# Sparse attention with a gated feed-forward: key tiles that hold their own 64 keys first, with the neighbours' rims copied on chip

## The chip, the cores and the metric

One core of a Trainium2 chip. The time is the device time of one execution in microseconds (us), as a median over the fast runs. The clock that the matrix engine (TensorE) is granted differs between executions: its mean over one execution of the kernel before was 0.984 to 0.994 of full speed. The engines are VectorE (DVE in the profile), ScalarE (ACT), GpSimd (POOL) and SyncE (SP). TensorE is PE, and its weight loads are PEld.

## The reference, cut to what matters

```python
B, H, S, D = 4, 8, 768, 64;  block, window = 32, 16
k_sum = k.reshape(B, H, S // block, block, D).max(axis=3)       # block maxima
v_sum = v.reshape(B, H, S // block, block, D).mean(axis=3)      # block means
local  = q @ k.T / 8,   kept where |i - j| < window
coarse = q @ k_sum.T / 8 + log(block)
x = softmax([local, coarse]) @ [v, v_sum]                       # 3072 x 512, all heads side by side
y = x + sigmoid(x @ w_res) * ((gelu(x @ w_gate) * (x @ w_val)) @ w_out)
```

A query sees the 31 keys within 15 positions of it, and 24 block keys. The feed-forward (w_gate, w_val: 512 x 1536, w_out back) has nearly all the arithmetic.

## The kernel before

Queries go in tiles of 64. The key tile of a query tile therefore holds 96 keys, its own 64 and a rim of 16 on each side, and below these the 24 block keys. In the kernel before these 96 rows lie in their natural order, and they are loaded whole: each rim row is read from memory a second time.

```python
def v_window(b, t):
    lo, hi = max(0, t * QT - WIN), min(S, t * QT + QT + WIN)
    r0 = lo - (t * QT - WIN)
    return r0, r0 + hi - lo, v[b, :, lo:hi, :].rearrange("h p d -> p h d")

def v_loads(b):                                   # 12 loads, f32 to bf16, issued by GpSimd
    for t in range(NT):
        r0, r1, src = v_window(b, t)
        nc.gpsimd.dma_start(out=vext[b % 2][r0:r1, t, :, 0:D], in_=src)

def k_place(b, hp, tp):                           # batches 0 and 1: tp is the turned k in PSUM
    nc.scalar.copy(<tiles 1..10 of kW, 96 keys each>, <tp>)
    nc.vector.tensor_copy(<tile 0>, <tp>);  nc.vector.tensor_copy(<tile 11>, <tp>)
    k_blocks(b, hp)                               # maxima by VectorE, then their copy into kW (L207)

def vsum_mm(b, vs, lo, hi):                       # block means of batch 0 on TensorE
    for t in range(lo, hi):
        for i in range(2):
            nc.tensor.matmul(vs[i][96:128, 0:DM // 2], bmat[:, t, :], vext[b % 2][0:BAND, t, 4*i:4*i+4, 0:D], ...)
```

The head of the kernel (batch 0, first half) turns k and q, makes four score tiles s with their exp P, makes the block means vs, copies them into vext (`vsum_head`), makes the four attention products ao, and then the first gate matmul g can run. keep_warm are idle matmuls that hold up the clock. The body (`fo_step`) makes g and vv for each of 12 columns of the feed-forward, and `res_step` and `ffn_step` make r and f. In odd units of a batch, the next batch is prepared inside these steps:

```python
for fo in range(0 if u else 2, FO):
    fo_step(st, gvT, fo)
    ...
    if half == 1 and nb < B:
        if fo == (4 if nb == 1 else 0):
            vsum_grp(nb, ps_t, "t")               # means: matmul, cast, four small copies by SyncE
            for i in range(4):
                vsum_bc(nb, 3 * i, 3 * i + 3, nc.gpsimd)      # into vext, GpSimd, 1.47 us each
        if nb == 1:
            if fo < NP: k_step(nb, fo, ps_t, "t") # turn k on TensorE, place it, maxima
        elif 4 <= fo < 4 + NP:
            k_blocks(nb, fo - 4)                  # maxima of batches 2 and 3
```

The softmax here doesn't subtract the row's maximum and nothing guards it: scores larger than these inputs give would overflow.

## Time and profile before

| | |
|---|---|
| time, median of 4 runs | 279.42 us (279.06 to 280.24) |
| span in the profiled run | 278.3 us |
| TensorE busy | 95% |
| first s, first ao, first g | 11.66, 21.26, 25.64 us |
| granted clock from 17.7 to 24.5 us | half |

A line of the timeline has the start, the length, the engine, the source line, and what was written and read; the bracket at its end says how long the engine sat idle before it and what released it. Such waits on TensorE, once the g and vv matmuls run back to back, are what can be saved. In the first 26 us everything can be saved that lies on the way to the first g. The lines are in the prediction.

### The profile page before, as it was taken

Reading aid. Unit: us, or ns where it says so; the run is one execution under the profiler, and the core shown is the slowest. Engines: PE = TensorE matmul, PEld = TensorE weight load, DVE = VectorE, ACT = ScalarE, POOL = GpSimd, SP = SyncE. Lnnn points to the kernel's source line nnn. Section 1 sums busy time; section 2 is a strip of 40 time slices with the busy share of each in tenths; the row PEclk is TensorE's granted clock in tenths of the full one; section 3 lists DMA queues with packets and bytes.
Section 4 is the critical chain, followed back from the end, with each engine's and each line's share of the span. In section 5 each row is a group of like instructions: output and inputs, shape, how many; then the busy total and the mean of one; then the engine's idle time right before and its main releaser. Section 6 shows DMA issues by size and latency. Waiting matters only on the chain.

```text
span 278.3 us, 5822 instructions
## 1 busy us (share of the span) xinstructions
PE 265.1 (95%) x2370; PEld 143.4 (52%) x2370; DVE 163.3 (59%) x366; ACT 129.8 (47%) x204; POOL 103.5 (37%) x130
## 2 busy tenths in 40 slices
PE   6879999999999999999899999999899999999994
PEld 2435554554544555455445565455454565556543
DVE  5847433599337633575956833685947743683424
ACT  1865447475466445543254445443255336343320
POOL 7986763520499962001999820001600000000000
PEclk9977999999999999999999999999999999999999
DMA  5999999994069999971199999311001100111003
GB/s 89 171 175 196 196 206 207 157 159 107 4 41 147 172 152 121 158 134 41 10 115 152 179 172 156 95 46 44 0 0 40 75 2 0 39 40 40 0 0 114
DMA packets 99818, 27.51 MB, mean 99 GB/s; under 512 B 83720, under 2 KB 96848, under 8 KB 99792
## 3 DMA queue, kind: packets, MB, share of 16 engines
q0 software_dynamic: 80560, 16.85, 69.6%
q1 hardware_dynamic: 19232, 10.30, 18.4%
q8 instruction: 18, 0.29, 0.4%
q14 instruction: 8, 0.07, 0.1%
HBM read 33.69 MB, written 6.29 MB: 144 GB/s over the span
## 4 chain that ended last, share of the span: by engine, by line
PE 83%; DVE 6%; DMA 5%; issue 2%; ACT 1%; POOL 1%; POOLq 0%; DVEq 0%
PE g L312 21%; PE f L344 21%; PE vv L312 20%; PE r L334 8%; PE ao L290 4%; PE s L272 3%; DMA q_sb<-in_q_dram 3%; PE xp L301 2%; DMA vext<-in_v_dram 2%; DVE ks L203 2%; DVE gvT L318 2%; PE tp L229 1%; PE f L365 1%; PE wp L373 1%; PE vs L250 1%
## 5 line engine op out<-in xcount | busy, mean ns | idle before, releaser
L318 DVE TENSOR_TENSOR gvT<-ge,vv 128x384 bf16<-128x384 f32 x96 | 52.6, 552 | 56.6 <-PE vv L312 56.1
L317 ACT ACTIVATE ge<-g 128x384 f32<-128x384 f32 x96 | 47.1, 491 | 82.6 <-DVE gvT L318 42.9
L312 PE MATMUL vv<-xT,w_val 128*128 128x384 bf16 x384 | 78.4, 326 | 2.8 <-DVE gvT L318 2.7
L312 PE MATMUL g<-xT,w_gate 128*128 128x384 bf16 x384 | 80.0, 326 | 0.1
L344 PE MATMUL f<-w_out,gvT 128*128 128x512 bf16 x276 | 65.5, 379 | 0.0
L312 PEld LDWEIGHTS <-w_val 128*128 128x128 bf16 x384 | 37.5, 98 | 29.0 <-issue 4.9
L312 PEld LDWEIGHTS <-w_gate 128*128 128x128 bf16 x384 | 35.7, 98 | 24.5 <-issue 2.5
L262 POOL COPY vext<-vsum 32x1536 bf16<-32x1536 bf16 x14 | 20.0, 1465 | 72.4 <-DMA vsum<-vpart 72.3
L276 ACT ACTIVATE P<-s,bias_t 128x768 bf16<-128x768 f32 x32 | 28.9, 902 | 31.9 <-PE s L272 31.7
L112 POOL DMA_DIRECT2D vext<-in_v_dram x48 | 36.6, 780 | 16.7 <-DMA w_out<-in_moe_w_out_dram 5.3
L344 PEld LDWEIGHTS <-gvT 128*128 128x128 bf16 x276 | 26.1, 98 | 29.3
L279 DVE TENSOR_TENSOR P<-P,maskt 128x768 bf16<-128x768 bf16 x32 | 17.8, 556 | 21.0 <-ACT P L276 20.9
L334 PE MATMUL r<-w_res,xT 128*128 128x512 bf16 x96 | 24.3, 380 | 0.0
L350 DVE SCALAR_TENSOR_TENSOR th<-th,f 128x512 f32<-128x512 f32 (+1 forms) x25 | 16.4, 658 | 6.1 <-PE f L344 5.8
L296 DVE TENSOR_TENSOR xn<-ao,rz 128x384 bf16<-128x384 f32 x32 | 17.8, 557 | 1.1
L120 POOL DMA_DIRECT2D k_nat<-in_k_dram x24 | 18.1, 768 | 0.0
L352 DVE SCALAR_TENSOR_TENSOR o<-th,xn 128x512 f32<-128x512 f32 (+1 forms) x25 | 16.8, 670 | 0.9
L294 DVE RECIPROCAL rz<-ao 128x6 f32<-128x6 f32 x32 | 6.2, 192 | 17.2 <-PE ao L290 17.2
L290 PEld LDWEIGHTS <-P 128*64 128x64 bf16 x384 | 9.0, 114 | 13.8 <-DVE P L279 6.4
L337 ACT ACTIVATE th<-r 128x512 f32<-128x512 f32 x24 | 14.2, 595 | 3.4 <-PE r L334 2.9
L203 DVE TENSOR_REDUCE ks<-kW 128x24 bf16<-128x768 bf16 x16 | 15.2, 948 | 0.3
L290 PE MATMUL ao<-vext,P 128*64 128x65 bf16 x384 | 12.6, 203 | 0.0
(71 smaller groups left out, 187.2 us busy)
## 6 DMA issues: line engine op xcount, KB each, us to landing
out_dram<-o SPq DMA_DIRECT2D x23, 256.0 KB
vext<-in_v_dram POOLq DMA_DIRECT2D x40, 96.0 KB, 6.6
k_nat<-in_k_dram POOLq DMA_DIRECT2D x20, 96.0 KB, 3.8
q_sb<-in_q_dram POOLq DMA_DIRECT2D x4, 384.0 KB, 8.6
w_gate<-in_moe_w_gate_dram POOLq DMA_DIRECT2D x6, 256.0 KB, 8.1
w_val<-in_moe_w_val_dram POOLq DMA_DIRECT2D x6, 256.0 KB, 8.7
w_out<-in_moe_w_out_dram POOLq DMA_DIRECT2D x3, 512.0 KB, 14.7
q_nat<-in_q_dram POOLq DMA_DIRECT2D x12, 128.0 KB, 6.0
```

What stands on the lines that cost most here:

```text
L112: nc.gpsimd.dma_start(out=vext[b % 2][r0:r1, t, :, 0:D], in_=src)
L120: nc.gpsimd.dma_start(out=k_nat[r0:r0 + hi - lo, t].rearrange("p (h d) -> p h d", d=D), in_=k[b, :, lo:hi, :].rearrange("h p d -> p h d"))
L203: nc.vector.tensor_reduce(out=ks.rearrange("d (t n) -> d t n", n=2), in_=kw[:, :, WIN:WIN + QT].rearrange("d t (n w) -> d t n w", w=BLK), ...
L262: eng.tensor_copy(vext[b % 2][96:128, lo:hi, :, 0:D], src)
L276: nc.scalar.activation(P.rearrange("p a t q -> p a (t q)"), s[:, :, 0:TU], AF.Exp, scale=scale, bias=bias_t[:])
L279: nc.vector.tensor_mul(Pf, Pf, maskt.unsqueeze(1).to_broadcast([128, 2 * HT, QT]))
L290: nc.tensor.matmul(ao[64 * e:64 * e + 64, sub, hh, :], P[:, hh, t, :], vext[b % 2][:, half * HT + t, 2 * hp + hh, 0:D + 1], start=True, st ...
L312: nc.tensor.matmul(ps[:, 0:TU], w[:, ko, fo * 128:(fo + 1) * 128], st["xT"][:, ko, :], start=(ko == 0), stop=(ko == KO - 1), skip_group_ch ...
L317: nc.scalar.activation(ge[:], g[:, 0:TU], AF.Gelu)
L318: nc.vector.tensor_mul(gvT[:, fo, :], ge[:], vv[:, 0:TU])
L334: nc.tensor.matmul(r[:], st["xT"][:, ko, ss], w_res[:, ko, :], start=(ko == 0), stop=(ko == KO - 1))
L344: nc.tensor.matmul(st["f", sub][:], gvT[:, fo, ss], w_out[:, fo, :], start=(fo == 0), stop=(fo == FO - 1), skip_group_check=True)
```

## The change

Its intent: to load each row of v and k once. The tiles hold their own 64 keys first (rows 0 to 63), and the two rims behind them (64 to 79 the following tile's first 16, 80 to 95 the preceding tile's last 16). The rims are copied on the chip. Since own rows start at row 0, the means need 64 rows only. The head's fillers are rearranged too.

```diff
-            nc.gpsimd.dma_start(out=vext[b % 2][r0:r1, t, :, 0:D], in_=src)
+            nc.gpsimd.dma_start(out=vext[b % 2][0:QT, t, :, 0:D], in_=v[b, :, t * QT:(t + 1) * QT, :]...)
+    def v_rims(b, lo, hi):
+        x = vext[b % 2]; a, e = min(hi, NT - 1), max(lo, 1)
+        nc.sync.dma_start(out=x[QT:QT + WIN, lo:a, :, 0:D], in_=x[0:WIN, lo + 1:a + 1, :, 0:D])
+        nc.sync.dma_start(out=x[QT + WIN:BAND, e:hi, :, 0:D], in_=x[QT - WIN:QT, e - 1:hi - 1, :, 0:D])
 # head: two of the mask's selects become four, and go behind the loads
-        <2 affine_selects on maskt, 2 on bpair>
         v_loads(0)
+        <4 affine_selects on maskt>
+        v_rims(0, 0, HT);  v_rims(0, HT, NT)
 # k of batches 0 and 1
-            nc.scalar.copy(<tiles 1..10, 96 keys>, <tp>)
-            nc.vector.tensor_copy(<tile 0>, <tp>);  nc.vector.tensor_copy(<tile 11>, <tp>)
-            k_blocks(b, hp)
+            nc.scalar.copy(kW[b % 2][:, :, hp, 0:QT]..., <tp, all 12 tiles, 64 keys>)
+            k_blocks(b, hp)
+            k_rims(b, slice(hp, hp + 1), nc.vector)          # two copies inside kW
 # k of batches 2 and 3: smaller load and DMA transpose, then
+                    k_rims(nb, slice(0, NP), nc.gpsimd)
 # means
-                                     vext[b % 2][0:BAND, t, 4 * i:4 * i + 4, 0:D],
+                                     vext[b % 2][0:QT, t, 4 * i:4 * i + 4, 0:D],
 # TensorE's order in the head
         vsum_mm(0, vs, 2, 5)
+        fill(2)
         s_step(0, 2, st)
+        fill(2)
         vsum_mm(0, vs, 5, 8)
+        fill(2)
         s_step(0, 3, st)
 ...
-        keep_warm(2); av_step(0, 0, st); keep_warm(2); av_step(0, 1, st, ps_mm, "mm"); keep_warm(1)
+        fill(3); av_step(0, 0, st, ps_mm, "mm"); fill(2); av_step(0, 1, st); fill(1)
 # later batches, in odd units, gate step 0
+                        v_rims(nb, 0, NT)
```

## The prediction

> **What bounds the kernel now.** I read the page first, then the busy table by stretches, the chain of waits, and the timelines of single engines where the chain leaves TensorE.
>
> ```profile
> span 278.3 us, 5822 instructions
> PE 265.1 (95%) x2370; PEld 143.4 (52%) x2370; DVE 163.3 (59%) x366; ACT 129.8 (47%) x204; POOL 103.5 (37%) x130
> ...
> PE   6879999999999999999899999999899999999994
> ...
> PEclk9977999999999999999999999999999999999999
> DMA  5999999994069999971199999311001100111003
> ```
>
> TensorE is the bound from slice 4 (28 us) to the end, and its matmuls there (g, vv, f, r) are untouched. Time can come only from the first 26 us, before the first g matmul, and from later places where TensorE waits. The table of stretches shows the start:
>
> ```profile
> core 0: us, PE busy (x) PEld busy (x) DVE busy (x) ACT busy (x) POOL busy (x), PEclk, DMA share, GB/s
> 10.90:14.30 3.40, 2.94 (x58) 1.97 (x59) 3.23 (x10) 3.29 (x6) 3.40 (x5) 1.00 2.41 153
> 14.30:17.70 3.40, 1.52 (x22) 0.92 (x20) 1.55 (x3) 1.77 (x3) 2.54 (x4) 1.00 2.33 160
> 17.70:21.10 3.40, 3.29 (x24) 1.44 (x22) 1.43 (x4) 2.72 (x4) 3.37 (x5) 0.50 1.50 194
> 21.10:24.50 3.40, 3.40 (x43) 1.73 (x42) 2.04 (x5) 1.94 (x4) 2.24 (x4) 0.50 1.45 195
> ```
>
> TensorE is busy 45% from 14.3 to 17.7 and then runs at half clock for 6.8 us. The timeline of TensorE says why, and the chain of waits confirms it (6.58 us of waiting on a v load, ending at 18.88):
>
> ```profile
> 17.47 0.38 PE L237 MATMUL vs<-vext,bmat 96*32 96x256 bf16 x2 [1.72 <-DMA vext<-in_v_dram]
> 17.78 0.50 PE L272 MATMUL s<-qT,kW 64*128 64x64 bf16 x12
> 18.24 2.13 PE L237 MATMUL vs<-vext,bmat 96*32 96x256 bf16 x8
> 20.30 1.03 PE L373 MATMUL wp<-warm 128*128 128x512 bf16 x2
> 21.26 0.54 PE L290 MATMUL ao<-vext,P 128*64 128x65 bf16 x12
> ...
> 25.64 0.49 PE L312 MATMUL g<-xT,w_gate 128*128 128x384 bf16 x2
> ```
>
> Block means need all 12 v tiles, and these land late. From GpSimd's timeline, the first seven v loads follow q at once; the eighth waits:
>
> ```profile
> 10.78 3.82 POOL L112 DMA_DIRECT2D vext<-in_v_dram  x5 [0.59 <-DMA q_sb<-in_q_dram]
> ```
>
> Later, TensorE waits in two kinds of place: some 0.24 us after each of four k turns of batch 1 (59 to 67 us), and 1.37 us at 136 and at 198:
>
> ```profile
> 61.12 0.53 PE L196 MATMUL tp<-ident,k_sb 96*64 96x96 bf16 x16 [0.24 <-DVE kW L220]
> 137.73 0.81 PE L312 MATMUL vv<-xT,w_val 128*128 128x384 bf16 x4 [1.37 <-DVE gvT L318]
> ```
>
> **What the Trainium skill says.** "TensorE: Matmul & The Clock Gate", part 1, says that the array drops to half clock after an idle window of about 3.4 us and comes back after a busy one. The trace agrees in kind: 0.50 for 6.8 us after a poorly filled stretch (it was not fully idle). "DMA: Bandwidth & Descriptors", "Queues, rings and completion order", says that each DMA engine takes turns between its queues by packets; so copies from SyncE share with loads from GpSimd. No run so far shows the size. "SBUF — State Buffer", "SBUF: two separate sides", says that VectorE and GpSimd lock each other out of a shared port pair. The trace agrees: the VectorE copy L207 takes 0.23 us alone and 1.21 and 1.48 us while GpSimd copies vext (131.4 to 137.1). Its "Door 1: The DMA port swizzle" puts a 64-partition load at 196 GB/s against more for wider ones; v moves at 154 now, so I expect no new limit.
>
> **The change, part by part.**
>
> *v loads.* A load shrinks from 96 to 64 rows, 98 KB to 65.5 KB written. From 10 to 17 us the queues move 154 GB/s, 0.64 us per old load; at the same rate a new one takes 0.43 us. Data of the 12 starts at about 10 us (q lands at 10.5). Old: 1147 KB / 154 = 7.45 us, so 17.4, and the last landing is about 19.4 (the load whose landing ends the chain's wait at 18.88 was issued at 12.30; the last went out at 13.85, and no load took under 5.6 us from issue to landing). New: 786 KB / 154 = 5.1 us, so 15.1. GpSimd still issues the last five from 10.78 at 0.76 us each, so the last is out at 14.6: about the same limit. With the 2 us that landing trailed the data before, the last v is there at about 17.1, plus up to 0.6 us from the rim copies in the queues: 17.1 to 17.7.
>
> *Rims of v.* Two SyncE copies per half, about 700 pieces of 128 B each, 44 per DMA engine. Old v loads took 48 pieces per engine in 0.64 us, so I estimate 0.6 us per copy alone and 1.2 shared. Tile seven lands at about 14.5; issue 0.66 us each (the time of a vsum copy on that queue), about 1.6 us to land (vsum copies: last issue ends 72.1, reader starts 73.7): 17.5 to 18. The first attention product needs the first half only. So rims just miss being the path.
>
> *Means and softmax side.* Old: vs ends at 20.30, ao starts at 21.26 (0.96 later: cast 0.43, first head 0.36, hand-overs). New: vs ends at 17.3 to 17.9. But the fourth s waits for tile eight (I put it at 15.5), two fillers and 0.35 us of s, then exp 0.90 and mask 0.56, so VectorE is free for the cast at about 17.9: ao at 18.7 to 18.9. The mask is made after the v issues now (four selects of 0.25 us from 14.6, ready at 15.6), so three mask products run at 15.6 to 17.2: hidden. Gain to here: 21.26 - 18.8 = 2.45 us.
>
> *Clock.* Six new fillers of 512 columns (0.22 us at full clock, 0.43 at half) stand at 14 to 17 us. 1.3 us of them in 3.4, plus 1.5 us of other work, makes about 80%, as in 10.9 to 14.3, which wasn't throttled. From ao to g took 4.38 us at half clock. At full clock VectorE's chain sets it: ao 0.38, then rz plus xn at 0.76 each, three of them, 0.6 us of hand-overs and xp: 3.2 us. Gain 1.2 us. The fillers behind vs (3 x 0.22 = 0.65) fit in the 0.96 us gap.
>
> Start in sum: 2.45 + 1.2 = 3.65. I weigh in one chance in five that the clock drops all the same (minus 1.2 or more): 3.4 us.
>
> *Do the weights follow?* w_res is there at about 39.9 and w_out's first third at 42.4 (GpSimd's waits end then), needed at 43.4 and 45.2. A start 3.6 us earlier needs them at 39.8 and 41.6. Their queue moves up by 1 to 2.3 us (fewer v bytes, minus rims). 38.3 and 40.7 would do; the margin is under 1 us.
>
> *k of batch 1.* Two copies from PSUM (0.15 us of VectorE's pace each, 0.23 long) go; two rim copies of 176 elements come, estimated 0.12 each against 0.15 to 0.23 for the 288 of L207. What matters more: the turned tile is now read by ScalarE alone (768 columns instead of 960, an estimated 0.78 us instead of 0.96), so TensorE's next turn no longer waits on VectorE's L220. VectorE's pace goes from 2.02 to about 1.84 us per step, TensorE's work is 1.77. Four waits of 0.24 go: 0.9 us.
>
> *k of batches 2 and 3.* Load and DMA transpose shrink by a third (12.35 and 9.2 us before), both hidden. Rims are two GpSimd copies of 704 elements per partition, at 1465 ns / 1536 elements an estimated 0.7 us each; they come near 108 us, when GpSimd has finished its loads, with nothing waiting. The block maxima on VectorE are the same size, and GpSimd's vext copies still collide with them: the two 1.37 us waits stay. Later v rims precede vsum's copies on SyncE and may push the collision by 1 us or so: 0 +- 0.8.
>
> Sum: 3.4 + 0.9 + 0 = 4.3 us, 279.6 to 275.3.
>
> **Rivals.**
> (a) The rim copies take the place of the v landing: SyncE copies queued among weight loads land after 19 us. For it: piece count hardly falls (2944 removed, 2816 added), and the queues are saturated. Against it: the first half needs only seven tiles. Gain at the start then 1.5 to 2: about 277.
> (b) The clock still drops, because the remaining waits on tiles 8 and 12 fall into one window. Fillers speak against it. About 276.8.
> (c) The weights become the bound in 35 to 46 us and give 1 us back: 276.3. The narrow margins speak for it, the 8-deep issue ahead against it.
> (d) The collisions at 133 and 195 shift out of the maxima entirely: 1.37 twice, about 272.7. It needs some 5 us of delay for vsum, which 2.4 us of rim traffic don't give.
>
> **Range and chances.** Errors of 1 us in landing, 0.8 in clock, 0.8 in collisions, 0.3 in k add up to about 1.6 us, more towards less gain. Predicted 275.3 us, range 273.7 to 277.5. 2% would be 274.0: faster by over 2% 0.15, within 2% 0.82, slower by over 2% 0.03.
>
> **What would show it.** Right: first g at about 22 us; clock 1.00 through 14 to 25; vs done before 18; no wait on L220 and none of 0.24 us at 56 to 64; waits of about 1.4 us before vv twice, DMA transpose of k near 8 and 6 us; TensorE without gaps at 35 to 46. Wrong: an ao waiting on a vext copy from SyncE (a), clock 0.50 (b), r or f waiting on w_res or w_out (c), or only one or no such wait before vv (d). A slower kernel would need the rims to hold ao past 21 us.

## The result, and the profile after

| | before | after |
|---|---|---|
| time, median of 4 runs | 279.42 us | 277.89 us (277.64 to 278.24) |
| ratio, 95% interval | | 0.9942 (0.9916 to 0.9969) |
| span in the profiled run | 278.3 us | 276.5 us |
| first ao, first g, first f | 21.26, 25.64, 45.17 us | 20.04, 23.23, 44.08 us |

A ratio is the mean time of one kernel's fast runs over that of the other's of the same rounds, so not quite the ratio of the medians quoted. Executions over 1.5% slower than the fastest of the same kernel are left out of the means. The gain is 1.5 us (0.6%, clear of noise) where 4.3 was forecast; 277.89 us lies just above the forecast range. Two rows of the page come first, the granted clock and the DMA share in 40 slices of the span:

```profile
PEclk9999999999999999999999999999999999999999
DMA  5999999999089999104099997104001100111003
```

The clock does not fall in this run. The busy table of the same stretches as before (columns: the stretch, TensorE, its weight loads, VectorE, ScalarE, GpSimd, clock, DMA share, GB/s):

```profile
10.90:14.30 3.40, 2.88 (x59) 1.92 (x58) 2.67 (x8) 3.33 (x6) 3.40 (x6) 1.00 2.21 143
14.30:17.70 3.40, 3.24 (x41) 1.52 (x40) 1.58 (x3) 1.59 (x4) 3.21 (x8) 1.00 1.22 113
17.70:21.10 3.40, 2.53 (x36) 1.42 (x35) 2.40 (x6) 3.31 (x5) 3.40 (x5) 1.00 1.31 158
21.10:24.50 3.40, 3.16 (x56) 2.01 (x49) 2.92 (x11) 2.55 (x6) 2.37 (x4) 1.00 1.59 196
```

Two things are to be read. TensorE is busy 95% from 14.3 to 17.7 where it was 45%: it no longer waits for v, and part of the time is now filled with idle matmuls (wp below). And the last column: before, the queues moved 160 and 194 GB/s in the two middle stretches, now 113 and 158. Less data was asked for, and the queues did not use the room. The timeline of TensorE:

```profile
16.71 0.61 PE L393 MATMUL wp<-warm 128*128 128x512 bf16 x2
17.25 0.35 PE L267 MATMUL s<-qT,kW 64*128 64x64 bf16 x12
17.53 1.04 PE L232 MATMUL vs<-vext,bmat 64*32 64x256 bf16 x8
18.50 0.82 PE L393 MATMUL wp<-warm 128*128 128x512 bf16 x3
20.04 0.38 PE L285 MATMUL ao<-vext,P 128*64 128x65 bf16 x12 [0.71 <-DVE vext L238]
...
23.23 0.49 PE L307 MATMUL g<-xT,w_gate 128*128 128x384 bf16 x2
...
36.15 0.36 PE L224 MATMUL tp<-ident,q_sb 96*64 96x96 bf16 x8 [0.82 <-DMA q_sb<-in_q_dram]
...
44.08 1.90 PE L339 MATMUL f<-w_out,gvT 128*128 128x512 bf16 x8 [0.29 <-DMA w_out<-in_moe_w_out_dram]
```

No bracket on vs, so v is there when TensorE comes to it. The fourth s at 17.25 stands behind fillers (wp). And at 36.15 and 44.08 stand waits on loads that the kernel before does not have. From the first g to the first f TensorE took 45.17 - 25.64 = 19.53 us before and takes 44.08 - 23.23 = 20.85 now: of 2.41 us gained at g, 1.32 are given back. The larger of the two named waits, 0.82 us, is on the second half's q, whose load GpSimd issues between the weights. GpSimd's own waits tell when weights land (before it issues another load it is seen waiting for an old one). Before:

```profile
40.16 0.77 POOL L112 DMA_DIRECT2D vext<-in_v_dram  x1 [1.73 <-DMA w_res<-in_moe_w_res_dram]
42.70 0.77 POOL L112 DMA_DIRECT2D vext<-in_v_dram  x1 [1.77 <-DMA w_out<-in_moe_w_out_dram]
```

After, with the mask's selects ahead of the first weight:

```profile
14.05 1.18 POOL L164 TENSOR_SCALAR_AFFINE_SELECT maskt<-maskt 64x64 bf16<-64x64 bf16 x4
15.22 0.77 POOL L177 DMA_DIRECT2D w_gate<-in_moe_w_gate_dram  x1
...
42.08 0.68 POOL L104 DMA_DIRECT2D vext<-in_v_dram  x1 [2.29 <-DMA w_res<-in_moe_w_res_dram]
44.31 0.68 POOL L104 DMA_DIRECT2D vext<-in_v_dram  x1 [1.56 <-DMA w_out<-in_moe_w_out_dram]
```

So the weights land 1.9 and 1.6 us later than before, although 360 KB less of v stood ahead of them. As many bytes of rim copies came in their place, and yet the queues moved less in all: from 13 to 22 us, 137 GB/s on average where it was 175. In the later stages, the maxima of batch 2:

```profile
133.02 5.72 POOL L257 COPY vext<-vsum 32x1536 bf16<-32x1536 bf16 x4 [24.29 <-DMA vsum<-vpart]
```

```profile
136.52 0.81 PE L307 MATMUL g<-xT,w_gate 128*128 128x384 bf16 x4 [0.23 <-DVE gvT L313]
139.34 0.81 PE L307 MATMUL g<-xT,w_gate 128*128 128x384 bf16 x4 [1.37 <-DVE gvT L313]
```

Counted from the means matmul of that stage, GpSimd's copies start 133.02 - 123.65 = 9.37 us in, where they started 131.43 - 125.50 = 5.93 us in before. SyncE, which issues the rims and then the four copies of the means, shows why. Before and after:

```profile
127.21 2.85 SPq L256 DMA_DIRECT2D vsum<-vpart  x4
```

```profile
126.37 5.30 SPq L251 DMA_DIRECT2D vsum<-vpart  x4
```

The copies of the means start 2.72 us after the means matmul instead of 1.71, behind two rim copies, and take 5.30 us instead of 2.85. GpSimd's copies then collide with other maxima than before, at the same price: from the means matmul to the next unit's first s the two stages took 16.88 and 16.80 us before and take 17.09 and 16.80.

### The profile page after: what moved, and what is told of

The parts are those of the page before. It is cut to its first block, busy times and chain, and to the rows that moved or that the text cites. A ratio compares the mean times of both kernels' runs of the same rounds, so it can differ in the third digit from the quotient of the medians.

```text
span 276.5 us, 5854 instructions
## 1 busy us (share of the span) xinstructions
PE 262.2 (95%) x2352; PEld 142.7 (52%) x2377; DVE 161.9 (59%) x365; ACT 128.7 (47%) x204; POOL 101.2 (37%) x134
## 4 chain that ended last, share of the span: by engine, by line
PE 75%; DMA 11%; DVE 4%; POOL 4%; issue 3%; ACT 1%; POOLq 0%; DVEq 0%
PE f L339 20%; PE g L307 19%; PE vv L307 18%; PE r L329 7%; DMA w_out<-in_moe_w_out_dram 5%; DMA w_gate<-in_moe_w_gate_dram 4%; PE ao L285 3%; PE s L267 3%; DMA q_sb<-in_q_dram 3%; PE xp L296 2%; DVE ks L199 2%; DVE gvT L313 2%; POOL vext L104 1%; PE f L360 1%; PE tp L224 1%
## 5 line engine op out<-in xcount | busy, mean ns | idle before, releaser
L339 PE MATMUL f<-w_out,gvT 128*128 128x512 bf16 x262 | 62.6, 379 | 1.6 <-issue 1.0
L104 POOL DMA_DIRECT2D vext<-in_v_dram x48 | 33.1, 761 | 13.3 <-DMA w_out<-in_moe_w_out_dram 5.3
L274 DVE TENSOR_TENSOR P<-P,maskt 128x768 bf16<-128x768 bf16 x32 | 17.7, 556 | 20.6 <-ACT P L271 18.9
L117 POOL DMA_DIRECT2D k_nat<-in_k_dram x24 | 16.4, 746 | 0.0
```

Of the source, the lines that this page charges most:

```text
L104: nc.gpsimd.dma_start(out=vext[b % 2][0:QT, t, :, 0:D], in_=v[b, :, t * QT:(t + 1) * QT, :].rearrange("h p d -> p h d"))
L274: nc.vector.tensor_mul(Pf, Pf, maskt.unsqueeze(1).to_broadcast([128, 2 * HT, QT]))
L339: nc.tensor.matmul(st["f", sub][:], gvT[:, fo, ss], w_out[:, fo, :], start=(fo == 0), stop=(fo == FO - 1), skip_group_check=True)
```

## The experiments

All ratios are against runs of the kernel before on the same chip in the same rounds. The interval is 95%. Where medians of two experiments are compared, they can come from different chips, on which the kernel before took 279.3 to 279.6 us. Each landing time is that of one profiled execution. Runs 3, 5 and 6 leave the loads of the head as the change has them, and there GpSimd's waits on w_res and w_out end at 41.21, 41.70 and 41.81, and at 43.73, 43.94 and 44.35 us, against 42.08 and 44.31 in the profile after. So a landing time is sure to about 0.9 us only.

**1. Without the rim copies of v in batch 0.** Wrong result on purpose: ScalarE zeroes those rows early.

```diff
+        nc.scalar.copy(vext[0][QT:BAND, :, :, 0:D], <zeros>)
-        v_rims(0, 0, HT);  v_rims(0, HT, NT)
```

> The changed kernel without the two pairs of on-chip rim copies of batch 0 (those rows zeroed by ScalarE early, so the result is wrong on purpose). Theory 1, the rim copies' traffic holds up the weight loads: the second q load and w_res, w_out land 1.2 to 2.5 us earlier than in the changed kernel (w_out's first third at 41.5 to 42.8 instead of 44.0), TensorE's wait of 0.8 us before the first turn of the second q half goes, and the span is about 1.2 us shorter: near 276.5 us against 277.9. Theory 2, the queue runs dry because GpSimd issues the first weight late (15.22, after four mask selects): weights move by under 0.5 us and the time stays at 277.5 to 278.

Measured: ratio 0.9935 (0.9906 to 0.9964), median 277.84 us, but six runs from 276.12 to 280.82, the longest of them slow. GpSimd's waits on w_res and w_out end at 41.05 and 43.59, so 1.0 and 0.7 us earlier than in the profile after: more than theory 2 allowed and less than theory 1 asked. The wait of 0.8 us for the second half's q is gone, and the span is 0.9 us shorter. But against run 3, which keeps the rims and issues its first weight at the same time (15.02 against 15.01), the weights come only 0.16 and 0.14 us earlier: what the rims alone cost is not settled. The busy table of this run by single microseconds shows the other half of it:

```profile
13.00:14.00 1.00, 0.44 (x20) 0.39 (x19) 0.97 (x4) 0.93 (x3) 1.00 (x3) 1.00 2.29 157
14.00:15.00 1.00, 1.00 (x15) 0.66 (x12) 1.00 (x2) 1.00 (x2) 0.81 (x4) 1.00 1.38 83
15.00:16.00 1.00, 1.00 (x16) 0.34 (x14) 0.96 (x6) 0.40 (x2) 1.00 (x3) 1.00 1.12 71
16.00:17.00 1.00, 1.00 (x8) 0.48 (x7) 0.73 (x3) 0.72 (x1) 1.00 (x2) 1.00 0.40 25
17.00:18.00 1.00, 1.00 (x17) 0.51 (x17) 0.31 (x1) 0.07 (x1) 1.00 (x3) 1.00 1.36 183
```

With the rims gone nothing hides it: the small v loads are through by 16 (about 1980 KB have moved by then; k, q and v have 1966), the first weight was issued from 15.01 to 15.78, and from 16 to 17 the queues move 25 GB/s. The queue runs dry. By the same count the larger v loads of the kernel before last until about 17, and the first weight was issued at 14.59.

**2. The mask's selects ahead of the v loads.**

```diff
         q_sb[0] = load_q(0, 0)
+        <4 affine_selects on maskt>
         v_loads(0)
-        <4 affine_selects on maskt>
```

> The changed kernel with GpSimd's four mask selects ahead of the v loads instead of behind them (where the kernel before has its selects). Theory 2 (queue dry for want of issue): first weight issued about 1.2 us earlier, at 14.0, w_out's first third lands at 42.8 to 43.2 instead of 44.0, waits at 36 and 44 us shrink, time about 277.0. Theory 1 (rim traffic): nothing moves at 36 to 44, 277.9.

Measured: the first weight is issued at 13.86, and the waits end at 41.06 and 43.60: again 1.0 and 0.7 us earlier than in the profile after, in the direction of theory 2, but again only 0.15 and 0.13 earlier than in run 3. The time did not follow: ratio 0.9977 (0.9945 to 1.001), runs from 277.6 to 280.8. In the profiled run ao waited 0.27 us on a rim copy, and the clock fell to 0.54 from 21.1 to 24.5. That weights which come earlier stand beside the rims in the queues is a guess, not shown. So theory 2 may be right on the weights, its time was missed, and the clock is less safe than the profile after suggested.

**3. Without the six fillers.**

```diff
-        fill(2)
         s_step(0, 2, st)
-        fill(2)
         vsum_mm(0, vs, 5, 8)
-        fill(2)
         s_step(0, 3, st)
```

> The changed kernel without the six fillers between the third and the fourth s. Theory 3, the fillers now stand on TensorE's path and made ao start at 20.0 instead of the predicted 18.8: ao at 19.0 to 19.4; and the clock stays 1.00 since v lands early enough. If instead the v tiles set it, ao stays near 20.0, and the clock falls to 0.50 for one or two windows. Either way the time moves little, 277.5 to 278.5, if the weights bind from 36 us on.

Measured: ratio 0.9946 (0.9933 to 0.996), 278.10 us. The profiled run, at full clock:

```profile
18.53 0.38 PE L285 MATMUL ao<-vext,P 128*64 128x65 bf16 x12 [0.41 <-DVE vext L238]
...
21.62 0.49 PE L307 MATMUL g<-xT,w_gate 128*128 128x384 bf16 x2
...
25.65 0.82 PE L307 MATMUL vv<-xT,w_val 128*128 128x384 bf16 x4 [0.37 <-DMA w_val<-in_moe_w_val_dram]
...
35.74 0.36 PE L224 MATMUL tp<-ident,q_sb 96*64 96x96 bf16 x8 [1.16 <-DMA q_sb<-in_q_dram]
```

ao starts 1.5 us earlier than in the changed kernel, and earlier than expected, and g 1.6. No wait for v shows on TensorE in the head even so. So the fillers stood on TensorE's path. But the first f came at 43.49, only 0.6 earlier, because TensorE now waits on loads, and in three of the five runs the clock averaged 0.984 to 0.987, as it does in most runs of the kernel before (the changed kernel, and runs 5 and 6 with the same head: 0.997 to 1.0 in all 13). In these runs the fillers do buy the clock, at 1.5 us; the time is the same without them (277.89 and 278.10).

**4. The kernel before, with only the changed kernel's TensorE order in the head.** Loads, key order and k as before.

> The kernel before with only the changed kernel's TensorE order in the head (nine more fillers of 512 columns and the swapped accumulators), loads and key order as before. If the clock is what the change gains at the start: clock 1.00 from 17.7 on, first g at 23.9 to 24.6 instead of 25.6, time about 278.2 (ratio 0.995), so as good as the whole change there. If the smaller v loads are what gains: still the wait on v until 17.5, g no earlier than 25, time 279.0 or more.

(It has seven more fillers; the text above miscounts.) Measured: ratio 0.9948 (0.9936 to 0.996), 278.01 us, at a mean clock of 0.998 to 1.0 in all five. That is as much as the whole effect of the change (0.9942), without the key order. Fillers and swapped accumulators were not tried apart. From its profile:

```profile
18.88 0.62 PE L237 MATMUL vs<-vext,bmat 96*32 96x256 bf16 x4 [0.19 <-DMA vext<-in_v_dram]
...
20.50 0.38 PE L290 MATMUL ao<-vext,P 128*64 128x65 bf16 x12 [0.24 <-DVE vext L243]
...
23.59 0.49 PE L312 MATMUL g<-xT,w_gate 128*128 128x384 bf16 x2
```

The wait on v shrank to 0.19 us, and g comes 0.36 us after the changed kernel's. f comes at 43.12, 0.96 before the changed kernel's, since the weights are not late here. What the key order earns later, with k of batch 1 (0.76 us), brings it level.

**5. The rims of k from PSUM.** In batches 0 and 1, VectorE takes them from the turned tile instead of from the placed keys.

```diff
-            k_rims(b, slice(hp, hp + 1), nc.vector)
+            nc.vector.tensor_copy(<first rims of kW>, tp.rearrange("d j (t p) -> d t p j", t=NT)[:, 1:NT, 0:2])
+            nc.vector.tensor_copy(<second rims>, tp.rearrange("d j (t p) -> d t p j", t=NT)[:, 0:NT - 1, 6:8])
```

> The changed kernel, but the rims of k in batches 0 and 1 are copied by VectorE from the turned tile in PSUM, as the kernel before does with its edge tiles, instead of from the placed keys. Theory: in batch 1 the changed kernel lost the four waits of 0.24 us because TensorE's next turn no longer waits for VectorE. Then the waits come back, at 176 elements per copy a little longer: 0.2 to 0.5 us each, 0.8 to 2 us in all between 57 and 66 us, time 278.7 to 279.8. If the gain came from the shorter ScalarE copy instead, no waits come back and the time is 277.9 plus at most 0.3.

Measured: ratio 1.015 (1.0134 to 1.0166), 283.69 us, 5.8 more than the changed kernel. The direction is as expected, the size is a miss:

```profile
60.84 0.53 PE L192 MATMUL tp<-ident,k_sb 96*64 96x96 bf16 x16 [1.41 <-DVE kW L219]
```

The waits are 1.41, 1.24, 1.24 and 1.24 us. My edit put the copies behind the maxima, so the PSUM tile stays held for the maxima too; in the kernel before the PSUM copies came first and held it less long (0.24 at the first turn). VectorE itself idles 1.00 us in each of the last three steps here, so its load is not the cause: who reads the turned tile last can set TensorE's next turn. In the kernel before, VectorE works without a pause from the second step on and takes 2.02 us for one; in the changed kernel it takes 1.82. How much of the old waits was its load, and how much the held tile, stays open.

**6. The maxima of batches 2 and 3 three steps earlier.**

```diff
-                    elif 4 <= fo < 4 + NP:
-                        k_blocks(nb, fo - 4)
+                    elif 1 <= fo < 1 + NP:
+                        k_blocks(nb, fo - 1)
```

> The changed kernel with the block maxima of batches 2 and 3 taken in the steps 1 to 4 instead of 4 to 7, so before GpSimd's copies into vext start. Theory: the two waits of TensorE there (1.6 and 1.0 us) come from VectorE's copy L203 being locked out by those copies. Then L203 takes 0.23 us in all eight places, the waits go to under 0.3 us each, and the time falls by 2 to 2.6 us to 275.3 to 275.9. If VectorE's sheer work makes the waits, they stay, and so does 277.9.

Measured: ratio 0.9825 (0.9806 to 0.9843), 274.70 us, and correct. No wait on TensorE is left in these stages, and the copy of the maxima takes 0.23 to 0.24 us in all eight places. From the means matmul to the next first s each stage takes 15.17 us instead of 17.09 and 16.80, which is 3.55 us in sum. That is more than the named waits (1.60 and 1.02) and more than expected: most of the rest is time that the profile counts as busy (15.49 and 15.64 us of TensorE in the changed kernel, 15.17 in both stages here, for the same matmuls). So GpSimd's copies blocked VectorE's, as the Trainium skill says that these two engines do in "SBUF — State Buffer", "SBUF: two separate sides": a VectorE copy that met GpSimd's copies took up to 1.48 us instead of 0.23, which is 1.25 more, a little under the 1.43 of one GpSimd copy. The last maxima end at 132.5; GpSimd's copies begin at

```profile
132.95 5.71 POOL L257 COPY vext<-vsum 32x1536 bf16<-32x1536 bf16 x4 [24.39 <-DMA vsum<-vpart]
```

**7 and 9. Runs 1 and 2 together, twice.**

> Runs 1 and 2 together: no rim copies of v in batch 0 (wrong result on purpose) and the mask selects ahead of the v loads. Each alone brought w_res about 1.0 us and w_out's first third about 0.7 us forward. If they are two separate causes, together they bring nearly the sum: the GpSimd waits on w_res and w_out end at 40.0 to 40.4 and 42.6 to 43.0 instead of 42.1 and 44.3, as in the kernel before or a little earlier. If both act on the same bottleneck (a queue that holds nothing from 14 to 17 us), no more than one of them: 41.0 and 43.6.

> Run 7's kernel once more, because its profile fell in the state with the lower clock. GpSimd's waits on w_res and w_out end where run 7 had them (39.7 and 42.2)[...]; if this execution keeps full clock, no TensorE wait on a load from 20 to 50 us and a span near 274.5.

Measured: the waits on w_res and w_out end at 39.66 and 42.20 in the first profile, 40.14 and 42.68 in the second. (Run 9 is a single execution.) That is about the sum, as in the kernel before, and clear of the scatter of the landing times. But both profiles fell in executions at half clock from about 14 to 25 us (mean clock 0.976), so I take it as a sign that the two causes add, not as proof. The timed runs are of two kinds: 275.8, 276.12 and 276.18 at full clock, and 279.26, 279.33 and 280.82 at a lower one (ratio 0.9919). At full clock that is 1.7 to 2.1 us less than the changed kernel takes, with spans of 274.1 to 274.5. Run 9 did not keep full clock, so the condition of its expectation was not met.

**8. The kernel before with runs 4 and 6.** TensorE's order in the head and early maxima, without the key order.

> The kernel before with the two things that helped apart from the key order: the changed kernel's TensorE order in the head (run 4) and the block maxima in steps 1 to 4 (run 6). Without the key order it keeps the four waits of 0.24 us on the k turns, but its weights come early. If run 4's 0.52% and run 6's gain of about 3 us add, 275.2 us, within 0.3% of run 6 (274.7): then the key order is worth next to nothing here. If the key order matters for the maxima (the rims now on GpSimd), 276 or more.

Measured: ratio 0.9892 (0.9877 to 0.9906), 276.56 us: a miss against 275.2. The two do not simply add:

```profile
129.48 5.70 POOL L262 COPY vext<-vsum 32x1536 bf16<-32x1536 bf16 x4 [21.32 <-DMA vsum<-vpart]
...
132.39 1.47 DVE L207 COPY kW<-ks 128x288 bf16<-128x288 bf16 x1
```

Without the rim copies, the means arrive early and GpSimd's copies start at 129.48, in the midst of the maxima, whose last copy then takes 1.47 us instead of 0.23. The stages take 16.12 and 16.05 us here, 1.83 more than run 6's in sum, about the whole difference between the two medians (1.86). With the early maxima, the key order is worth 0.9892 - 0.9825 = 0.7% after all, by the delay of 3.4 us that its rims bring to the means. That is luck, not the aim of the key order: an obvious rival, run 8 with the means simply made later, was not tried.

**10. A combination.** Run 6, with the selects first and the second half's rims of batch 0 issued by ScalarE in gate steps 3 and 5.

> A try to beat run 6 (274.7): its early maxima, the mask selects first, and the second half's rim copies issued by ScalarE in the gate steps 3 and 5, when TensorE has work, instead of by SyncE behind the v loads. Weights should come 1.2 to 1.5 us earlier than in the changed kernel (w_res 40.6 to 40.9, w_out 42.8 to 43.1). If the clock holds, 273.6 to 274.2; if it falls as in run 2 (where ao waited on the first half's rims), 275 to 276.

Measured: ratio 0.9826 (0.9803 to 0.985), median 274.41 us, runs from 273.66 to 275.45. The weights came 1.0 and 0.7 us earlier than in the profile after (41.06 and 43.61), a little later than expected, and the profiled run has a span of 272.3 against 273.0 in run 6, but two of six runs lost some clock (0.991, 0.994). So it is level with run 6. These two are the fastest versions found, 1.2% ahead of the changed kernel.

## Why the prediction was wrong, point by point

| step | forecast | measured |
|---|---|---|
| v no longer awaited | last v at 17.1 to 17.7 | SyncE's wait on v ends at 17.1; no TensorE wait on v |
| first ao | 18.7 to 18.9 | 20.04; 18.53 in run 3 |
| clock | full | full |
| ao to g | 3.2 us | 3.19 us |
| weights | 1 to 2.3 us earlier | 1.9 and 1.6 us later |
| k of batch 1 | 0.9 us gained | 0.76 us gained |
| second half's q | not listed | TensorE waits 0.82 us for it |
| later stages | 0 +- 0.8 us | 0.2 us lost |

**The head.** The mechanism was right and a term was too small. I let the fillers run "at 14 to 17 us" to fill idle time, set the fourth s by the landing of the eighth v tile, and counted two fillers behind it. In fact TensorE had no idle time left there; six fillers of 0.22 us stood in its order ahead of that s, and its exp and mask came before VectorE's cast of the means: the s ran at 17.25, and the cast at 19.16 where I had 17.9. Run 3, without them, has ao at 18.53 and g at 21.62, where the prediction put them (though its clock held in only two of five executions). The cost of the omission is 1.2 us at ao.

**The weights.** This step failed in its sign. "Their queue moves up by 1 to 2.3 us (fewer v bytes, minus rims)" takes it for granted that the queue is never empty: it counts bytes at a fixed rate. The runs show the opposite: the weights landed 1.9 and 1.6 us later, because the queues moved 137 GB/s from 13 to 22 us instead of 175. Smaller v loads were through before GpSimd, at 0.7 to 0.8 us per issue and with four selects in between, had given the queues a weight. Run 1 shows the hole (25 GB/s at 16 us). The selects' order (run 2) and the rims (run 1) each brought the weights 1.0 and 0.7 us forward against the profile after, but 0.1 to 0.2 against run 3, so the share of each is not settled. Both together (runs 7 and 9) brought them back to where the kernel before has them, which is clear of the scatter. The prediction's rivals (a), rims in the queues, and (c), weights as the bound, were the right ones to name; I gave them 277 and 276.3, and they came together. Rival (a) has a wrong count: 2816 pieces are removed, not 2944, exactly as many as one batch's rims add. And the first wait to bind, that for the second half's q, is in none of the lists. Run 1 also has a second dip at 20 us (112 GB/s) with no rims in it; what makes it stays open.

**k of batch 1.** TensorE's wait on VectorE went, as told: between the first turn and the next unit's first s, 19.78 us became 19.02. Only the first of the four waits had 0.24 us in its bracket: from one turn to what follows it, the steps took 2.17, 2.02, 2.02 and 2.02 us and now take 1.86 to 1.87. Run 5 shows that a VectorE read of the turned tile can set the pace.

**The later stages.** The sum was right, in part by luck. The delay was mis-sized: I expected the collision to move by about 1 us, and it moved by 3.4. It fell on two other maxima out of four, so nothing was gained. The 0.2 us are not firm either: with the same code there, run 3 has 16.80 and 16.81 us. Rival (d) said that a shift out of the maxima would be worth about 2.7 us but needed 5 us of delay. Run 6 made the same thing from the other side, and was worth 3.2 us. The delay is that of the rims in SyncE's order (1.0 us) and of the slower means copies behind them (5.30 us instead of 2.85), as its timeline shows; no run tests it alone.

**Where the expected gain went.** 3.65 us were expected at the first g (3.4 with the chance of a lower clock) and 2.41 came; at the first f 1.09 were left; 0.76 came from k; 0.2 were lost in the maxima: 1.6 us, against 1.8 between the two spans. And run 4 shows that TensorE's new order in the head (fillers and accumulators) is enough for nearly the whole gain there, without the smaller loads: the key order itself, against run 4, is level.

## What to carry to other kernels

In this kernel, bytes saved at the front of the load queue brought the weights no earlier, with the next load not yet issued and other copies in their place: look at GB/s by the microsecond, and at what the issuing engine does between loads. Fillers that hold the clock are instructions in TensorE's order like all others: once the wait that they filled was gone, they stood on the path here. When two engines lock each other out, move one by a few steps before you make either smaller: that one line was worth twice the whole change.

## What the Trainium skill lacked or had wrong

- "TensorE: Matmul & The Clock Gate", part 1, ties half clock to an idle window of about 3.4 us and full clock to a busy one. Here a stretch in which TensorE was busy 45% was enough to lose it (kernel before, 14.3 to 17.7 us), and it was not given back for a long time to a TensorE that was busy throughout: run 9 shows 3.40 of 3.40 us busy in three windows running, 14.3 to 24.5, at 0.50. So the profile's busy time did not tell the clock here, and what else decides it stays open. The page does say that the window runs freely; run 3's kernel kept full clock in two of five executions.
- No page says to keep a load queue from running dry. In run 1, with the v loads through, the first weight was issued from 15.01 to 15.78 us, and the queues moved 25 GB/s from 16 to 17 and 183 in the next microsecond.
- No page has the cost of on-chip copies in pieces of 128 B beside a stream of loads. Here two pairs of them (360 KB) and a first weight issued later brought the weights 1.9 and 1.6 us late together; the share of the copies is not settled.
